# Attention with memory slots and a mixture of experts on one core: another order for the opening, and the second batch's value weights placed later

## The chip, the cores and the metric

One Trainium2 chip, one of its cores. The metric is the device time of one execution in microseconds (us), as the median of several runs.

## The reference

Sizes: batch 8, 8 heads, 576 rows, head width 64, 32 memory slots; model width 512, 8 experts of inner width 1024. All in float32.

```python
a = softmax(phi, axis=2)                               # 8 x 8 x 576 x 32
k_m = einsum('bhsm,bhsd->bhmd', a, k)                  # memory keys
v_m = einsum('bhsm,bhsd->bhmd', a, v)                  # memory values
attn = softmax(q @ k_m^T / 8)
x = (attn @ v_m) as 4608 tokens x 512
logits = x @ w_gate + modality_bias[modality_id]
e = argmax(logits);  gate = softmax(logits)[e]
out = gate * (relu(x @ w1[e]) @ w2[e])                 # per token, its own expert
```

With these inputs the biases decide, and the kernel takes the expert that the first token prefers for all, checks at the end whether any token wanted another, and only then runs a slow path.

## The kernel before, in words

Work goes batch by batch. A batch's 576 tokens lie as 64 x 9 rows; part 0 is four of the nine row groups (`RA`), part 1 the other five (`RB`). The attention's last product is never made: memory values times w1 gives "value weights" (`value_products`, 128 x 1024 for each of two groups of heads), and the hidden layer is the softmax weights times these (`hidden`, eight pieces f = 0 to 7). For precision each operand is split in an upper and a lower half (`...h`, `...l`), and a product is three: upper by upper, lower by upper, upper by lower. `outputs` multiplies the hidden rows by w2, three products for each f, into one bank for each tile t of 128 tokens; `store` scales by the gate on ScalarE (`ob`) and writes out.

PSUM has eight banks: four in a ring under the name `pe`, and two pairs (`pair_of_banks(0)` and `(1)`; `bank("pa")` and `bank("mem")` are the first halves of these).

Order is by hand. `plan_first` writes the steps of batch 0's first part in the order in which they are issued. `plan_memory`, `plan_turns` and `plan_steps` put the attention steps of later batches in a list with due times, and `plan_experts` lists the expert steps. `weave` merges the two lists by a table of planned costs (`TAKES`): an attention step goes out when the steps that it names are done by plan, its `floor` is reached and its due progress is made; else the next expert step does. Within each list the order stays. Each engine works through its own instructions in the order issued, so a step that waits holds up what stands behind it on its engine.

The opening of batch 0, by engines: SP loads phi, k, the first part of q, v, then (when the first token's expert is known) w1, w2 and the rest. VectorE reduces the peaks (`first_max`), subtracts, ScalarE takes exponentials in two pieces of five and four rows (`mem_exp`), TensorE multiplies by k and then v (`first_products`), while VectorE sums the exponentials (`mem_sums`). `first_divide`, `first_even` and `first_odd` scale the even heads on ScalarE and the odd ones on VectorE. The keys are turned on TensorE (`first_keys`), q in place on VectorE (`q_turn`), then come the scores of part 0, the softmax (`soften`, `first_weights`) and the split of its weights (`first_split`, `xah` and `xal`) for each group of heads. Value weights of the first 512 columns are made twice (step `vw` 0 and 2): the second copy has the upper half taken off by TensorE (`value_rest`), and ScalarE writes the lower half (`value_remainder`); the other 512 columns are done by ScalarE (`value_upper`) and VectorE (`value_lower`). `warm` issues products that nobody reads. `first_w2` splits one of eight chunks of w2: ScalarE casts `w2h`, GpSimd subtracts `w2l`. The step `start` sets the planned clock.

The hidden pieces f = 0 to 3 of part 0 are made term by term (`some_hidden`, steps ha to he), f = 4 and 5 in the two halves of one pair of banks (`one_of_two`), the rest in ring banks. After that tiles 0 and 1 get their output products, the second scores come (part 1 of batch 0), and tiles 2 and 3 follow after part 1's hidden pieces. Batch 1's value weights stand behind tile 2 (first half) and in the middle of tile 3 (second half).

Of the kernel before, what the change touches and what calls it, by code (L numbers as in the profile page):

```python
# [8 lines left out]
F32 = mybir.dt.float32  # L9
# [45 lines left out]
def attn_moe(ctx: ExitStack, tc: tile.TileContext, q, k, v, phi, mod_id, w_gate, mod_bias, w1, w2, out):  # L55
# [23 lines left out]
    BUSY = 86, 10  # L79
# [74 lines left out]
    def warm(n, small=False, name="pa"):  # L154
        if n > 0:
            idle = pair_of_banks(0) if small else bank(name)
            for n in range(n):
                if small:
                    r, c = QP * (n % 2), BL * (n // 2 % 4)
                    nc.tensor.matmul(  # L160
                        idle[c:c + BL, n % 2, 0:16], lhsT=busy[r:r + QP, 0:BL], rhs=busy[r:r + QP, 0:16],
                        start=True, stop=True, tile_position=(r, c),
                    )
                else:
                    nc.tensor.matmul(idle, lhsT=busy[:, 0:P], rhs=busy, start=True, stop=True)


# [88 lines left out]
    def biases(pairs):  # L256

        for pair in pairs:
            for m in range(NMOD):
                ts_ = slice(pair * QC, (pair + 1) * QC)  # L260
                part = wk.tile([P, QC, E], F32, name="part") if m else bias[:, pair]
                nc.gpsimd.tensor_tensor(
                    part, is_m[m][:, ts_].broadcast_to([P, QC, E]), mb[:, m:m + 1, :].broadcast_to([P, QC, E]),
                    op=ALU.mult,
                )
                if m:
                    nc.gpsimd.tensor_tensor(bias[:, pair], bias[:, pair], part, op=ALU.add)
# [67 lines left out]
    def mem_exp(b):  # L335
# [6 lines left out]
        else:  # L342
            topc = live["topc", b]
            pb = bank("mem")
# [6 lines left out]
        for cs in (slice(0, RB), slice(RB, QC)):  # L351
            nc.vector.tensor_tensor(
                px[:, :, cs], ph[:, :, cs], peak.broadcast_to([P, HG, cs.stop - cs.start, M]), op=ALU.subtract
            )
            nc.scalar.activation(px[:, :, cs], px[:, :, cs], AF.Exp)
        live["pe", b] = pe, None

    def mem_sums(b):
        pe = live["pe", b][0]
        if b == 0:  # L360
            x = pe.rearrange("p j x -> p (j x)")
            t2 = wk.tile([P, HG, 4 * M], F32, name="t2top").rearrange("p j x -> p (j x)")
# [371 lines left out]
    def value_upper(hf):  # L734
        for g, pv in enumerate(live["pv", hf]):
            nc.scalar.copy(vws[0][:, g, hf * 512:(hf + 1) * 512], pv)
# [13 lines left out]

    def value_weights(b, hf):
# [4 lines left out]
    def hidden(i, part, f, terms=range(3), groups=range(NG), to=None):  # L756
# [16 lines left out]
        if terms[-1] < 2 or groups[-1] < NG - 1:  # L773
            return
# [4 lines left out]
        for p0, p1, h0 in parts:  # L779
            hh, hl = (x[:, f, h0:h0 + p1 - p0] for x in hs)  # L780
            nc.vector.scalar_tensor_tensor(hl, ph[:, p0:p1], 0.0, hh.bitcast(F32), op0=ALU.max, op1=ALU.subtract)  # L781
# [49 lines left out]
    def first_w2(c):  # L831
# [15 lines left out]
        "vwp": (1.15, ""), "vwu": (0.0, "A1.15"), "vwl": (0.0, "D1.35"),  # L847
# [48 lines left out]
    def plan_first():  # L896
# [4 lines left out]
        def nothing(n, name="pa"):  # L901
            add(("nothing", len(attention)), "nothing", [], warm, n, False, name)
# [425 lines left out]
```

## Time and profile before

| | |
|---|---|
| median of 3 runs | 395.9 us (395.86 to 395.95) |
| profiled execution | 395.96 us, its span 394.1 us |
| busy: TensorE, VectorE, ScalarE, GpSimd | 380.2, 243.0, 144.9, 46.0 us |
| granted TensorE clock | 0.997 of full speed |
| moved by DMA | 56.91 MB |

The span is counted from the first to the last instruction. In the profile's views PE is TensorE, PEld its weight loads, DVE VectorE, ACT ScalarE, POOL GpSimd, SP the engine that issues most DMAs (`SPq` its queue). A row has start, length and engine, the source line (L798), the operation and what it writes and reads; "x16" stands for as many alike in a row, and square brackets hold idle time of the engine before and what ended it. A line is that of the listing above; helpers such as `turn` (L146) stand for many callers, so tiles tell more.

### The profile page before, as it was taken

The numbers are of one execution on the slowest core, as the hardware profiler recorded it, in microseconds if no ns is written. First come the engines' busy times: TensorE is split into PE (matmuls) and PEld (weight loads), VectorE is DVE, ScalarE is ACT, GpSimd is POOL, SyncE is SP. The second block draws the span as 40 slices with busy tenths as digits, with TensorE's granted clock in tenths as the row PEclk, the third lists the DMA queues.
The fourth block names the chain that finished last, engine by engine and source line by source line (L and its number), as shares of the span: only waits on it lengthen the run. The fifth ranks groups of instructions, "written<-read, shape, count | busy, mean of one in ns | idle before, by whom it ended". The sixth has DMA issues, their size and how long they took to land.

```text
span 394.1 us, 10127 instructions
## 1 busy us (share of the span) xinstructions
PE 380.2 (96%) x4217; PEld 305.0 (77%) x4219; DVE 243.0 (62%) x612; ACT 144.9 (37%) x347; POOL 46.0 (12%) x112
## 2 busy tenths in 40 slices
PE   7789999999999999999999999999999999999993
PEld 3557785889779887787878878797968879698982
DVE  4676864885797466856687366873687558660400
ACT  2264333515344333433443234352533425251410
POOL 3219420013000200030000200011000200000000
PEclk9999999999999999999999999999999999999998
DMA  8998167624841391628311293616211011431111
GB/s 291 360 380 311 66 163 280 245 108 140 260 140 46 106 368 57 227 77 303 112 27 55 62 346 118 218 30 210 86 28 28 27 30 29 167 128 28 30 33 55
DMA packets 28700, 56.91 MB, mean 144 GB/s; under 512 B 3044, under 2 KB 8164, under 8 KB 28644
## 3 DMA queue, kind: packets, MB, share of 16 engines
q1 hardware_dynamic: 28368, 55.87, 42.3%
q8 instruction: 35, 0.57, 0.6%
q10 hardware_dynamic: 276, 0.30, 0.2%
q14 instruction: 21, 0.17, 0.1%
HBM read 37.28 MB, written 18.87 MB: 142 GB/s over the span
## 4 chain that ended last, share of the span: by engine, by line
PE 89%; DVE 4%; DMA 3%; ACT 1%; issue 0%; SPq 0%; ACTq 0%
PE pe L798 50%; PE pe L769 25%; PE pair L386 4%; PE pe L728 4%; PE pair L562 3%; DMA kv_sb<-in_v_dram 3%; PE pair L675 1%; PE pair L146 1%; PE pe L411 1%; DVE a L595 0%; PE pair L728 0%; DVE a L589 0%; DVE hl L781 0%; ACT ob L811 0%; PE pair L539 0%
## 5 line engine op out<-in xcount | busy, mean ns | idle before, releaser
L798 PE MATMUL pe<-w2h,hh 128*128 128x512 f32 x288 | 116.8, 406 | 0.0
L798 PE MATMUL pe<-w2h,hl 128*128 128x512 f32 x288 | 112.5, 391 | 0.0
L798 PE MATMUL pe<-w2l,hh 128*128 128x512 f32 x288 | 110.4, 391 | 0.0
L781 DVE SCALAR_TENSOR_TENSOR hl<-pe,hh 128x256 fp32r<-128x256 f32 (+2 forms) x158 | 57.9, 392 | 42.1 <-ACT hh L778 41.2
L798 PEld LDWEIGHTS pe<-w2h,hh 128*128 128x128 f32 x288 | 54.1, 188 | 23.2 <-issue 12.3
L778 ACT ACTIVATE hh<-pe 128x256 fp32r<-128x256 f32 (+2 forms) x158 | 53.3, 362 | 37.9 <-PE pe L769 37.4
L798 PEld LDWEIGHTS pe<-w2l,hh 128*128 128x128 f32 x288 | 54.0, 188 | 11.8
L798 PEld LDWEIGHTS pe<-w2h,hl 128*128 128x128 f32 x288 | 54.2, 188 | 9.5
L811 ACT ACTIVATE ob<-pe,gates 128x512 f32<-128x512 f32 x36 | 24.8, 691 | 81.6 <-issue 49.0
L769 PE MATMUL pe<-xbh,vwh 128*128 128x320 f32 x128 | 40.1, 313 | 0.7 <-ACT ob L811 0.7
L769 PE MATMUL pe<-xbh,vwl 128*128 128x320 f32 x128 | 39.5, 309 | 0.0
L769 PE MATMUL pe<-xbl,vwh 128*128 128x320 f32 x128 | 39.5, 309 | 0.0
L769 PE MATMUL pe<-xah,vwh 128*128 128x256 f32 x124 | 34.5, 286 | 0.2 <-ACT xah L644 0.2
L769 PE MATMUL pe<-xal,vwh 128*128 128x256 f32 x124 | 34.5, 284 | 0.0
L769 PE MATMUL pe<-xah,vwl 128*128 128x256 f32 x124 | 34.5, 283 | 0.0
L322 POOL COPY ts<-tm 32x4 f32<-32x4 f32 x24 | 4.8, 199 | 201.3 <-DVE tm L314 200.5
L152 DVE TENSOR_TENSOR vwl<-pe,vwh 128x512 fp32r<-128x512 f32 x28 | 17.9, 679 | 13.0 <-ACT vwh L151 13.0
L589 DVE STREAM_TRANSPOSE a<-pair 128x256 f32<-128x256 f32 (+1 forms) x32 | 13.6, 461 | 18.9 <-PE pair L562 18.9
L769 PEld LDWEIGHTS pe<-xbh,vwh 128*128 128x128 f32 x128 | 24.0, 188 | 1.3 <-ACT ob L811 0.9
L769 PEld LDWEIGHTS pe<-xah,vwh 128*128 128x128 f32 x124 | 23.3, 191 | 1.9 <-ACT xah L644 1.6
L769 PEld LDWEIGHTS pe<-xbl,vwh 128*128 128x128 f32 x128 | 24.0, 188 | 0.3
L769 PEld LDWEIGHTS pe<-xbh,vwl 128*128 128x128 f32 x128 | 24.0, 188 | 0.0
(165 smaller groups left out, 459.0 us busy)
## 6 DMA issues: line engine op xcount, KB each, us to landing
kv_sb<-in_k_dram SPq DMA_DIRECT2D x8, 1152.0 KB, 5.7
kv_sb<-in_v_dram SPq DMA_DIRECT2D x8, 1152.0 KB, 9.4
out_dram<-ob SPq DMA_DIRECT2D x64, 128.0 KB, 2.4
q_sb<-in_q_dram SPq DMA_DIRECT2D x7, 1152.0 KB, 7.9
ph<-in_phi_dram SPq DMA_DIRECT2D x7, 576.0 KB, 4.1
raw<-in_moe_w_dram SPq DMA_DIRECT2D x2, 1024.0 KB, 7.6
raw<-in_moe_w_dram SPq DMA_DIRECT2D x1, 1280.0 KB, 10.5
out_dram<-ob SPq DMA_DIRECT2D x4, 256.0 KB, 2.6
```

The source lines that it names most:

```text
L146: nc.tensor.transpose(dst, src, ident[:rows, :rows])
L152: nc.vector.tensor_tensor(l, src, h.bitcast(F32), op=ALU.subtract)
L322: nc.gpsimd.tensor_copy(ts_[BL * a:BL * (a + 1)], live["tm"][BL * o:BL * (o + 1)])
L386: nc.tensor.matmul(live["kvp"][M * j:M * (j + 1), g], lhsT=pe[half, j, c * M:(c + 1) * M], rhs=kv_sb[half, :, j, c * D:(c + 1) * D], start ...
L562: nc.tensor.matmul(sc[g][M * j:M * (j + 1), a, c0 * BL:(c0 + n) * BL].rearrange("p (c t) -> p c t", t=BL), lhsT=kTs[b % 2][p0:p0 + BL, u, ...
L589: nc.vector.transpose(a[:, g].rearrange("p a c m -> p a (c m)"), sc[g][:, :, RA * part * BL:(RA * part + n) * BL])
L728: nc.tensor.matmul(pvs[g][M * j:M * (j + 1), :], lhsT=vT[b][rows, j, :], rhs=raw1[rows, j, cols], start=True, stop=not more, tile_position ...
L769: nc.tensor.matmul(ph[:, 0:n], lhsT=(vl if k == 2 else vh)[:, g, cols], rhs=xl if k == 1 else xh, start=(g == k == 0), stop=(g == NG - 1 a ...
L778: nc.scalar.activation(hs[0][:, f, h0:h0 + p1 - p0], ph[:, p0:p1], AF.Relu)
L781: nc.vector.scalar_tensor_tensor(hl, ph[:, p0:p1], 0.0, hh.bitcast(F32), op0=ALU.max, op1=ALU.subtract)
L798: nc.tensor.matmul(po, lhsT=tile_columns(hl if n == 1 else hh, f, t), rhs=(w2l if n == 2 else w2h)[:, f, :], start=(f == n == 0), stop=(f ...
L811: nc.scalar.activation(ob, po, AF.Copy, scale=gate_of(b, t))
```

## The change

- SP issues v's load ahead of the first part of q. Four more of the small products of nothing stand at the start.
- The first exponentials go by three rows in three pieces instead of five and four; their sums are added in thirds; the peaks that they subtract are spread into a ring bank instead of a pair.
- Four products of nothing instead of seven behind the exponentials, and three later in a ring bank instead of a pair; the spread of the known row moves ahead of k's products; the first turn of q moves behind the sums, ahead of the odd halves of the keys; v's products move behind it. Floors of several steps go.
- Value products stand behind the first group's softmax weights; the repeated ones are in ring banks; the split of the first weights comes ahead of the remainders; the upper halves of the second 512 columns are cast group by group around the second split, and the first chunk of w2 is split there too.
- Of the hidden pieces f = 0 to 3, two are in a pair of banks and evicted together (`relu`); f = 4 to 7 are all in ring banks. Tiles 0 and 1 take each chunk of w2 in turns.
- Biases of later pairs of batches are made one pair at a time, two batches apart. Batch 1's value weights move: the first half behind f = 1 of tile 3, the second to its end, with the lower half on VectorE after batch 1's first weights are split.

```diff
-    BUSY = 86, 10
+    BUSY = 90, 10
...
     def mem_exp(b):
...
-            pb = bank("mem")
+            pb = bank("mem" if b else "pe")
...
-        for cs in (slice(0, RB), slice(RB, QC)):
+        parts = [slice(c, c + QC // 3) for c in range(0, QC, QC // 3)] if b == 0 else (slice(0, RB), slice(RB, QC))
+        for cs in parts:
...
     def mem_sums(b):
...
-            nc.vector.tensor_tensor(t2, x[:, 0:4 * P], x[:, 4 * P:8 * P], op=ALU.add)
-            nc.vector.tensor_tensor(t2[:, 0:2 * P], t2[:, 0:2 * P], t2[:, 2 * P:4 * P], op=ALU.add)
+            nc.vector.tensor_tensor(t2, x[:, 0:n], x[:, n:2 * n], op=ALU.add)
+            nc.vector.tensor_tensor(t2, t2, x[:, 2 * n:3 * n], op=ALU.add)
             nc.vector.tensor_tensor(rf, t2[:, 0:P], t2[:, P:2 * P], op=ALU.add)
-            nc.vector.tensor_tensor(rf, rf, x[:, 8 * P:9 * P], op=ALU.add)
+            nc.vector.tensor_tensor(rf, rf, t2[:, 2 * P:3 * P], op=ALU.add)
...
+    def value_upper_weights(b, hf):
+        value_products(b, hf)
+        value_upper(hf)
...
+    def relu(i, part, fs):
+        n = MAIN + QP if part else MAIN
         parts = [(0, MAIN, 0), (MAIN, n, MAIN + QP)] if part and i else [(0, n, 0)]
-        for p0, p1, h0 in parts:
-            nc.scalar.activation(hs[0][:, f, h0:h0 + p1 - p0], ph[:, p0:p1], AF.Relu)
+        for f in fs:
+            for p0, p1, h0 in parts:
+                nc.scalar.activation(hs[0][:, f, h0:h0 + p1 - p0], live["ph", f][:, p0:p1], AF.Relu)
...
     def plan_first():
...
         def some_hidden(name, kind, after, terms, groups):
             for f in range(FCH // 2):
+                last_, own = terms[-1] == 2 and groups[-1] == NG - 1, f >= FCH // 4
...
+            if last_:
+                add(("h", 0, 0, FCH // 2 - 1), "relu", [], relu, 0, 0, range(FCH // 4, FCH // 2))
...
-        nothing(7)
+        nothing(4)
+        add(("known",), "nothing", [], spread_row)
+        add(("sums", 0), "first sums", [("exp", 0)], mem_sums, 0)
+        add(("k", 0), "k0", [("exp", 0)], first_products, 0, floor=9.0)
+        add(("ks", 0), "nothing", [("sums", 0)], first_sums)
+        add(("kn", 0), "kn0", [("k", 0), ("sums", 0)], first_divide)
         turns(0, 0, 9.5)
-        add(("sums", 0), "first sums", [("exp", 0)], mem_sums, 0)
-        add(("k", 0), "k0", [("exp", 0)], first_products, 0, floor=9.9)
-        add(("known",), "nothing", [], spread_row)
-        add(("ks", 0), "nothing", [("sums", 0)], first_sums)
-        add(("v", 0), "v0", [("exp", 0)], first_products, 1, floor=12.3)
-        add(("kn", 0), "kn0", [("k", 0), ("sums", 0)], first_divide)
         add(("ko", 0), "ko0", [("kn", 0)], first_odd, 0)
         turns(0, 1, 11.0)
+        add(("v", 0), "v0", [("exp", 0)], first_products, 1)
...
-        add(("vw", 0, 0), "vwp", [("kvT", 0)], value_products, 0, 0, pair_(0), floor=17.1)
-        add(("vw", 0, 2), "vwp", [], value_products, 0, 0, pair_(1), True, floor=18.2)
         add(("n", 0, 0, 0, 0), "n1", [("e", 0, 0, 0, 3)], first_weights, 0, 0)
-        add(("vwu", 0, 0), "vwu", [("vw", 0, 0)], value_upper, 0)
-        add(("vwr", 0, 0), "vwr", [("vwu", 0, 0)], value_rest, 0)
-        add(("vw", 0, 1), "vwp", [], value_products, 0, 1, pair_(0), floor=19.8)
         add(("n", 0, 0, 0, 1), "n2", [], first_weights, 0, 1)
         add(("e", 0, 0, 1, 2), "e1", [], soften, 0, 0, 2, 1)
-        add(("vwl", 0, 0, 0), "vw1", [("vwr", 0, 0)], value_remainder, 0, 0)
+        add(("vw", 0, 0), "vwp", [("kvT", 0)], value_products, 0, 0, pair_(0))
+        add(("vwu", 0, 0), "vwu", [("vw", 0, 0)], value_upper, 0)
+        add(("vw", 0, 2), "vwp", [], value_products, 0, 0, None, True)
         add(("xu", 0, 0, 0), "xu1", [("n", 0, 0, 0, 1)], first_split, 0, 0)
         add(("e", 0, 0, 1, 3), "ee", [("e", 0, 0, 1, 2)], soften, 0, 0, 3, 1)
         add(("xl", 0, 0, 0), "e1", [("xu", 0, 0, 0)], first_split, 0, 1)
+        add(("vwr", 0, 0), "vwr", [("vwu", 0, 0)], value_rest, 0)
+        for g in range(NG):
+            add(("vwl", 0, 0, g), "vw1", [("vwr", 0, 0)], value_remainder, 0, g)
+        add(("vw", 0, 1), "vwp", [], value_products, 0, 1, pair_(0))
...
-        add(("vwu", 0, 1), "vwu", [("vw", 0, 1)], value_upper, 1)
+        add(("vwu", 0, 1, 0), "vw1", [("vw", 0, 1)], value_upper, 1, range(1))
...
+        add(("vwu", 0, 1), "vw1", [("vw", 0, 1)], value_upper, 1, range(1, 2))
+        add(("w2", 0), "w2", [], first_w2, 0)
...
-        add(("start",), "start", [], lambda: None, floor=24.9)
+        add(("start",), "start", [], lambda: None, floor=25.0)
         turns(1, 0, 26.5)
-        turns(1, 1, 27.6)
-        add(("s", 0, 1), "s1", [("qt", 0, 1, 1), ("vwl", 0, 1)], scores, 0, RA, RB, floor=29.0)
+        turns(1, 1, 27.2)
+        add(("s", 0, 1), "s1", [("qt", 0, 1, 1), ("vwl", 0, 1)], scores, 0, RA, RB, floor=28.6)
...
     def plan_steps(b, dues):
...
-        if b == 0:
-            add(("bias", 1), "nothing", [], biases, range(1, NPAIR))
         if i:
             add(("others", pair), "others", [("g", b)], others, pair)
+            if b < B - 1:
+                add(("bias", pair + 1), "nothing", [], biases, pair + 1)
...
     def plan_experts(b):
...
-                if t == 2 and f == (FCH // 2 if b else FCH) - 1 or t == 3 and f == FCH // 2 - 1:
+                if b and t in (2, 3) and f == FCH // 2 - 1:
                     next_values(t - 2)
+                if b == 0 and t == 3 and f == 1:
+                    next_values(0)
+                if b == 0 and t == 3 and f == FCH - 1:
+                    stage(experts, ("vwp", 1, 1), "vwpu", [("kvT", 1)], value_upper_weights, 1, 1, banks=2, full=True)
+                    stage(experts, ("vw", 1, 1), "vwl", [("x", 1, 0), ("vwp", 1, 1)], value_lower, 1)
...
-                parts = [("o2", range(2), t, f) for t in tiles for f in range(FCH)]
+                parts = [("o2", range(2), t, f) for f in range(FCH) for t in tiles]
...
         load_kv(0, 0)
+        load_kv(0, 1)
         load_queries(0, 0, RA)
-        load_kv(0, 1)
-        warm(BUSY[0], True)
+        warm_small(BUSY[0])
         warm(BUSY[1])
```

More of the change, by code (lines that the diff above doesn't have):

```diff
@@ L152, in split, with warm, warm_small @@
         nc.vector.tensor_tensor(l, src, h.bitcast(F32), op=ALU.subtract)
[L154 to L165, printed above, removed]
+    def warm(n, name="pa"):
+        idle = bank(name)
+        for _ in range(n):
+            nc.tensor.matmul(idle, lhsT=busy[:, 0:P], rhs=busy, start=True, stop=True)
+    def warm_small(n):
+        idle = pair_of_banks(0)
+        for n in range(n):
+            r, c = QP * (n % 2), BL * (n // 2 % 4)
+            nc.tensor.matmul(
+                idle[c:c + BL, n % 2, 0:16], lhsT=busy[r:r + QP, 0:BL], rhs=busy[r:r + QP, 0:16],
+                start=True, stop=True, tile_position=(r, c),
+            )
     def halves(src, b):
@@ L254, in prepare, with biases @@
             nc.gpsimd.tensor_copy(wgd[rows, :, g, :], wg[rows])
[L256 to L267, printed above, removed]
+    def biases(pair):
+        for m in range(NMOD):
+            ts_ = slice(pair * QC, (pair + 1) * QC)
+            part = wk.tile([P, QC, E], F32, name="part") if m else bias[:, pair]
+            nc.gpsimd.tensor_tensor(
+                part, is_m[m][:, ts_].broadcast_to([P, QC, E]), mb[:, m:m + 1, :].broadcast_to([P, QC, E]),
+                op=ALU.mult,
+            )
+            if m:
+                nc.gpsimd.tensor_tensor(bias[:, pair], bias[:, pair], part, op=ALU.add)
     def rows_of(part):
@@ L754, in value_weights, with hidden @@
             split([x[:, g, hf * 512:(hf + 1) * 512] for x in vws], pv)
-    def hidden(i, part, f, terms=range(3), groups=range(NG), to=None):
+    def hidden(i, part, f, terms=range(3), groups=range(NG), to=None, evict=True):
         cols = slice(f * P, (f + 1) * P)
@@ L942, in plan_first @@
         add(("prepare",), "nothing", [], prepare)
-        add(("bias", 0), "nothing", [], biases, range(1))
+        add(("bias", 0), "nothing", [], biases, 0)
         for k in range(3):
@@ L1065, in plan_experts @@
                 kind = f"h{part + 2 * (part and b % 2)}"
-                own = b == part == 0 and f < FCH // 2 + 2
-                args = (range(3), range(NG), one_of_two) if own else ()
-                stage(
-                    experts, ("h", b, part, f), kind, [("x", b, part)] + ([("vwl", 0, 1)] if b == 0 else []),
-                    hidden, b % 2, part, f, *args, banks=int(not own), full=not own,
-                )
+                stage(experts, ("h", b, part, f), kind, [("x", b, part)] + ([("vwl", 0, 1)] if b == 0 else []), hidden, b % 2, part, f, banks=1, full=True)
                 if b == part == 0:
-                    for c in range(f - FCH // 2, f - FCH // 2 + 1):
-                        second(c)
+                    second(f - FCH // 2 + 1)
             tiles = range(2 * part, 2 * part + 2)
             if b == part == 0:
-                parts = [("o2", range(2), t, f) for t in tiles for f in range(FCH)]
+                parts = [("o2", range(2), t, f) for f in range(FCH) for t in tiles]
                 parts += [("o1", range(2, 3), t, f) for t in tiles for f in range(FCH - 1)]
@@ L1081, in plan_experts @@
                 for n, (kind, terms, t, f) in enumerate(parts):
[L1082 to L1083 removed]
+                    if n < FCH // 2 - 1:
+                        second(FCH // 2 + 1 + n)
                     some(t, f, kind, terms)
```

36 lines of the change are left out of this document (19 added, 17 removed), and 2 rows, old and new, of the table TAKES.

## The prediction

> **What bounds the kernel now.** I read the page first, then the chain of waits, the list of TensorE's waits, and last the rows in order of time where those waits stand.
>
> ```profile
> PE 380.2 (96%) x4217; PEld 305.0 (77%) x4219; DVE 243.0 (62%) x612; ACT 144.9 (37%) x347; POOL 46.0 (12%) x112
> PE   7789999999999999999999999999999999999993
> ```
>
> TensorE is busy 96% of 394.1 us. In the row of 40 slices (9.85 us each) only the first three and the last are below 9: in the opening a saved microsecond can end the kernel earlier, and from about 30 us on only a wait of TensorE itself counts. The profiled execution took 395.96 us, 1.86 more than its span; the median of the runs is 395.9, so the same difference holds for both.
>
> ```profile
> 2.28 11.43 DMA kv_sb<-in_v_dram
> 22.14 0.59 ACT vwl L744
> 30.01 1.44 PE pe L769 x12
> 34.86 1.09 PE pair L562 x57
> 46.91 0.70 ACT ob L811
> ```
>
> These are pieces of the chain that ended last (start, length, what; work between them left out). It is the load of v to 13.7, then a ping-pong of engines to 30, TensorE with products of the hidden layer (12 in 1.44 us, 0.12 each), the second part's scores at 34.86, then VectorE up to the first gated output, which ends at 47.6. Only behind that does TensorE run almost alone.
>
> ```profile
> PE pe L411 <- DMA kv_sb<-in_v_dram: 1.3, 1, 1.3
> PE pair L769 <- DVE hl L781: 0.9, 1, 0.9
> PE pair L562 <- ACT kT L512: 0.9, 2, 0.5
> PE pe L769 <- ACT ob L811: 0.7, 1, 0.7
> PE pair L146 <- ACT values L480: 0.4, 1, 0.4
> ```
>
> TensorE's waits (us in all, times, longest): 1.3 for v, 0.9 for a bank (`hl`, at 29 us), 0.7 for the first gated output (`ob`), and the two of 0.45 for batch 1's values and keys near 62 us. The change aims at all of them.
>
> **The loads.** SP now issues k, v, q; before it was k, q, v.
>
> ```profile
> L179 SPq DMA_DIRECT2D q_sb<-in_q_dram x1: 507/507/507, 1.7 to 1.7; - x1
> DMA to landing us min/median/max: 7.6/7.6/7.6
> ...
> L175 SPq DMA_DIRECT2D kv_sb<-in_k_dram x1: 454/454/454, 1.2 to 1.2; - x1
> L175 SPq DMA_DIRECT2D kv_sb<-in_v_dram x1: 698/698/698, 2.3 to 2.3; - x1
> DMA to landing us min/median/max: 6.6/9.0/11.4
> ...
> 10.00:11.00 1.00, 1.00 (x47) 1.00 (x40) 0.86 (x3) 0.12 (x1) 0.00 (x0) 1.00 1.11 403
> ```
>
> Issue times and times to landing: q 1.73 + 7.6 = 9.3; k 1.23 + 6.6 = 7.8; v 2.28 + 11.4 = 13.7. Between them the engines move about 403 GB/s (last row), so these loads queue behind one another. v without q's 512 KB ahead lands some 1.3 us sooner or more, at 12.4 or below. q becomes the last: at least 9.3 plus v's 1152 KB at that rate, 2.9, so 12.2; at most about 13.7, when now all four have landed. The gap of 1.4 us says that v's last packets were late for a reason that the queue's place alone doesn't give. I take 13.5, near the upper end, because that row measures the whole set. [...] No other DMA lies between these on SP, and what follows them comes in the same order as before.
>
> **Exponentials by three rows, and the order behind them.**
>
> ```profile
> 8.03 1.40 DVE L352 TENSOR_TENSOR exp<-ph,pair 128x640 f32<-128x640 f32 x2
> 8.86 1.26 ACT L355 ACTIVATE exp<-exp 128x640 f32<-128x640 f32 x2 [5.14 <-DVE exp L352]
> 9.68 2.19 PE L411 MATMUL pair<-kv_sb,exp 64*64 64x128 f32 x72
> 12.88 0.16 DVE L435 TENSOR_TENSOR recs<-rec,places 128x4 f32<-128x4 f32 x1
> 13.15 0.52 ACT L448 ACTIVATE even<-pair,recs 128x64 f32<-128x64 f32 x2 [0.74 <-DVE recs L435]
> 13.70 0.86 DVE L455 SCALAR_TENSOR_TENSOR keys<-pair,recs,even 128x64 f32<-128x64 f32 x4 [0.65 <-ACT even L448]
> 14.47 0.70 DVE L550 STREAM_TRANSPOSE q_sb<-q_sb 128x512 f32<-128x512 f32 x1
> 15.87 0.44 PE L146 MATMUL pair<-ident,keys 128*128 128x128 f32 x2
> 16.77 1.07 PE L562 MATMUL pair<-q_sb,kT 32*32 32x128 f32 x64 [0.46 <-ACT kT L512]
> ```
>
> Two subtractions take 1.40, two exponentials 1.26; one third of the nine rows costs about 0.53 and 0.49 (a half is 0.70 and 0.63, most of it by size). The products of k then start after 8.03 + 0.53 + 0.49 = 9.1 instead of 9.68, take 2.19 and end at 11.3; the last third is ready at about 10.1, before its turn. The peaks lie in a bank of their own, as the products would otherwise wait for the last subtraction to read them. The adds for the sums cost the same (three thirds for 512 and 256 columns), begin when VectorE has done the subtractions, without a turn of q ahead, and end near 11.3. So the reciprocals, 12.88 + 0.16 = 13.04 before, come at about 12.3, and the even halves at 12.9. Three fewer idle products and the four small ones more lie in TensorE's waits for data: nothing.
>
> The products of v follow on TensorE at about 11.7 (v is there or up to 0.7 late) and end by 13.9 to 14.6. But q's turn now stands on VectorE ahead of the keys, and it waits for q; behind it stand the odd halves, the second turn, and TensorE's turn of the keys. From q's landing: 0.70 + 0.86 + 0.90 (15.87 to 16.77) = 2.46; the second turn ends within that last piece. With 13.5 the first scores start at 15.97: **0.8 us** earlier. The ends are q at 13.7 (0.6) and q at 12.3 (2.0). The products of v leave the path.
>
> **First split and banks, to 27 us.**
>
> ```profile
> 21.33 0.45 DVE L638 STREAM_TRANSPOSE aT<-a 128x256 f32<-128x256 f32 x1
> 23.06 0.43 DVE L646 TENSOR_TENSOR xal<-aT,xah 128x256 fp32r<-128x256 f32 x1 [0.98 <-ACT xah L644]
> 25.67 0.42 DVE L646 TENSOR_TENSOR xal<-aT,xah 128x256 fp32r<-128x256 f32 x1 [0.47 <-ACT xah L644]
> 27.22 0.28 PE L769 MATMUL pair<-xah,vwh 128*128 128x256 f32 x1
> 29.03 0.38 PE L769 MATMUL pair<-xah,vwh 128*128 128x256 f32 x1 [0.93 <-DVE hl L781]
> 31.29 0.40 PE L798 MATMUL pe<-w2h,hh 128*128 128x512 f32 x1
> ```
>
> The first weights are turned at 21.78; ScalarE splits them only after a cast of `vwl` (22.14, chain), so VectorE idles 0.98 before 23.06. The new order splits first: 21.8 + 0.41, so VectorE goes on at 22.25, and the second group's weights, which wait for the second group's exponential behind it, move by nearly as much, as the cast no longer lies ahead of that exponential either; 0.1 goes to the exponential that they then wait for. The second split of 25.67 moves with them, since ScalarE's casts of `vwh` are now one ahead of it and one behind. **0.7 us**; between 0 (if the casts push it back) and 1.0, the longest such wait. Taking the repeated value products to banks of the other ring spares them the wait for the scores' transposes; what follows them waits for ScalarE's casts in any case, so nothing more.
>
> From 27.22 the hidden products of f = 4 to 7 stand: 31.29 - 27.22 = 4.07 for 24 products of 0.12, 2.9. The rest is the wait of 0.93 before 29.03, where both halves of the pair of banks hung on one reader, and small gaps. Now f = 2 and 3 sit in that pair, with both evictions after the last product, and f = 4 to 7 have ring banks, of which f = 5 needs that of f = 0, free in time if the evictions move up with the second split. **1.2 us**; 0 if VectorE's evictions come a product late each, 1.2 if not. The row of waits names one culprit, so I take the upper end.
>
> **w2.** The cast of the first chunk moves up on ScalarE, between the last cast of `vwh` and the first evictions, which have to wait for VectorE's `vwl` there anyway. Taking two tiles in turns uses a chunk every four output products; any small waits for casts go, and I count nothing. GpSimd starts its remainders earlier too.
>
> ```profile
> 31.02 5.04 POOL L829 TENSOR_TENSOR w2l<-raw,w2h 128x512 fp32r<-128x512 f32 x4 [0.62 <-ACT w2h L828]
> 37.77 1.46 DVE L595 TENSOR_TENSOR a<-a,mx 128x640 f32<-128x640 f32 x1
> ...
> 76.40 0.82 DVE L595 TENSOR_TENSOR a<-a,mx 128x640 f32<-128x640 f32 x1
> ```
>
> Four of these take 5.04, 1.26 each; eight need about 10.1, from about 25 on the new clock, so they end near 36, before the remainder products begin. They cost something where VectorE reads two operands from SBUF: 1.46 for a subtraction that takes 0.82 later on. That overlap of 0.64 exists already and stays; a second one would cost up to 1.26, none at best. I take none, as the instructions near the new start read PSUM. [...] The biases of later batches leave GpSimd's queue behind these for a place where it idles: nothing.
>
> **Part two and the gates.** So far 0.8 + 0.7 + 1.2 = 2.7 at the first output product. From the second scores (34.86) to the end of the gated output (47.61) are 12.75, mostly VectorE; the planner gives the scores 0.4 less floor, so they come after about the same count of output products or one pair fewer (0 to 0.46 earlier). TensorE's 0.7 at 47 shrinks by 0.2: **2.9** in all.
>
> **Batch 1.**
>
> ```profile
> 64.92 1.09 PE L728 MATMUL pe<-raw,vT 64*32 64x512 f32 x16
> ...
> 70.97 1.25 DVE L152 TENSOR_TENSOR vwl<-pe,vwh 128x512 fp32r<-128x512 f32 x2
> 72.14 0.68 DVE L658 TENSOR_TENSOR xal<-aT,xah 128x512 fp32r<-128x512 f32 x1
> ...
> 72.77 0.28 PE L769 MATMUL pe<-xah,vwh 128*128 128x256 f32 x1
> ```
>
> Its value products are put off: the first half behind two output steps of tile 3, the second to the end of that tile. The two waits near 62 us get work to fill them: 0.9. But batch 1's weights end at 72.14 + 0.68 = 72.82, and their first product starts at 72.77: no slack. Their cover from 64.92 is now 7.9 us; two output steps of 0.7 fewer make it about 6.4, while VectorE's chain loses only the 1.25 of the second half's remainder, now behind the weights. And that half needs two banks of four, one of which tile 3 gives back only by a gated output: up to 0.7 of new wait, like the one at 47. Between +0.9 and -0.8 I take **+0.2**, the middle, since the chain on VectorE shortens by about what its cover does.
>
> **Sum.** 2.9 + 0.2 = 3.1 against 395.96, that is 392.9, and 392.8 against the median.
>
> **The rivals.**
> *q lands early* (12.3). For it: 403 GB/s, and q's own 7.6 us. Against: v's 13.7. The first scores start 1.2 us earlier than forecast: 391.6. Chance 0.14.
> *VectorE gives it back.* GpSimd's remainders, now from about 25 us, block two more of VectorE's two-operand steps (0.64 each, by the subtraction's row), or evictions come late at f = 5 and 6. Then 1.3 of the 3.1 are lost: 394.1; with the bank wait of batch 1, 394.9. For it: no slack in VectorE's chain from 34.86 on. Chance 0.20. [...]
> *Nothing moves.* Another load (the first half of w1, or w2) would have to set the opening. The stream stays the same, and w2's first cast could be asked for too early; but the wait list names no such load. 395.9, chance 0.07.
> *Slower: batch 1's weights.* TensorE stands at batch 1's first hidden product until the weights are split, as its program has nothing else in between. The forecast turns at a wait of more than 3.1 + 0.2 us there, against none now; 0.8 more makes it measurable. At twice the loss of cover plus the bank and a blocked step (3.0 + 0.7 + 0.64) it is 397.0. For it: the slack of zero. Against: VectorE loses 1.25 of work in that stretch. Chance 0.07.
>
> **Numbers.** The forecast has 0.52, with its own range 392.0 to 393.7. Of 395.9, 0.2% is 0.8 us, about what the measurement can tell from no change. Faster: 0.52 + 0.14 + 0.20 = 0.86; same 0.07; slower 0.07. The range of 391.0 to 395.0 takes in the early q and the part given back and leaves out the last two.
>
> **What would show it.** v's products starting before 12.5 without a wait for DMA; a wait of VectorE for q at 12.3 to 13.6, ending in `q_sb`; first scores near 16.0; no 0.98 before `xal`; no 0.9 wait on `hl`; first output product near 28.6; first gated output ending near 44.7; near 60 us no waits for keys and values, and a wait or none at batch 1's first hidden product. It is wrong if q lands after 14.3 (then the scores start later than before), if the second scores don't move with the output products, or if TensorE stands for over a microsecond at batch 1.

## The result, and the profile after

The changed kernel takes 392.45 us (median of four runs, 392.29 to 393.04) against 395.88 before (four runs on the same chip): ratio 0.9917, 95% interval 0.990 to 0.9934. That is 3.4 us, of which 3.1 were forecast. The profiled execution took 392.55 us, its span 390.8. Of all runs told of below, one execution of `split_behind`, 420.05 us at a granted clock of 0.851, was slow and is left out.

The page of the changed kernel: busy times, and TensorE's row of 40 slices.

```profile
PE 379.2 (97%) x4218; PEld 305.1 (78%) x4220; DVE 243.7 (62%) x613; ACT 144.8 (37%) x348; POOL 45.7 (12%) x112
PE   7899999999999999999999999999999999999993
```

Of the 3.3 us by which the span is shorter, 2.3 were idle time of TensorE (11.6 instead of 13.9 us, gone from the first slices) and 1.0 counted as busy (379.2 for 380.2; the value products' gap, which comes below, counts as busy there). TensorE's waits, as in the list of before (us in all, times, longest):

```profile
PE pair L146 <- DVE keys L457: 0.7, 1, 0.7
PE pair L564 <- ACT kT L514: 0.5, 1, 0.5
PE pe L776 <- ACT xah L657: 0.4, 1, 0.4
PE pe L776 <- DVE xal L660: 0.3, 1, 0.3
PE pe L413 <- DMA kv_sb<-in_v_dram: 0.3, 1, 0.3
PE pair L396 <- POOL sums L283: 0.3, 1, 0.3
```

v's wait fell from 1.3 to 0.3; those for `hl`, for `ob` and for batch 1's values are gone. In their place stand a wait for the keys (VectorE now waits for q first), two at batch 1's first hidden product, 0.73 together, and one for `sums` of GpSimd (0.31, in batch 6, at 269 us). Rows of the changed kernel in order of time, from all engines (start, length, engine):

```profile
12.32 2.20 PE L413 MATMUL pe<-kv_sb,exp 64*64 64x128 f32 x72 [0.33 <-DMA kv_sb<-in_v_dram]
13.82 0.71 DVE L552 STREAM_TRANSPOSE q_sb<-q_sb 128x512 f32<-128x512 f32 x1 [1.20 <-DMA q_sb<-in_q_dram]
16.12 1.07 PE L564 MATMUL pair<-q_sb,kT 32*32 32x128 f32 x64 [0.46 <-ACT kT L514]
21.54 0.43 DVE L648 TENSOR_TENSOR xal<-aT,xah 128x256 fp32r<-128x256 f32 x1 [0.17 <-ACT xah L646]
25.70 0.28 PE L776 MATMUL pe<-xah,vwh 128*128 128x256 f32 x1
28.58 0.40 PE L812 MATMUL pe<-w2h,hh 128*128 128x512 f32 x1
30.97 1.18 PE L564 MATMUL pair<-q_sb,kT 32*32 32x160 f32 x64
33.95 1.85 DVE L597 TENSOR_TENSOR a<-a,mx 128x640 f32<-128x640 f32 x1
43.40 1.26 ACT L825 ACTIVATE ob<-pe,gates 128x512 f32<-128x512 f32 x2 [0.79 <-DVE gates L706]
69.06 0.39 PE L776 MATMUL pe<-xal,vwh 128*128 128x256 f32 x1 [0.34 <-DVE xal L660]
92.39 2.62 PE L388 MATMUL pair<-kv_sb,exp 64*32 64x128 f32 x141
```

Against the kernel before, the lead grows like this: first scores 0.65 us (16.77 to 16.12), first split 1.52 (23.06 to 21.54), hidden product of f = 4 also 1.52, first output product 2.71 (31.29 to 28.58), second scores 3.8 (34.79 to 30.97), first gated output 3.5 (46.91 to 43.40), batch 1's hidden products 3.8. Batch 2's first products start 3.8 earlier (96.18 to 92.39), but 141 of the 144 that took 2.25 now take 2.62, and the last of them ends 2.73 behind the first start. From batch 3 on the lead is 3.3; in batch 6 another 0.5 goes, and the last product of all starts at 384.29 instead of 387.13, 2.84 earlier. The rest of the span's 3.3 lies behind the last product, where the two executions took 6.48 and 6.96 us. That stretch took 6.4 to 7.2 us in the fourteen profiles of this case, in no order that I can see.

### The profile page after: what moved, and what is told of

It is laid out like the page before. It is cut to its first block, busy times and chain, and to the rows that moved or that the text cites. A ratio compares the mean times of both kernels' runs of the same rounds, so it can differ in the third digit from the quotient of the medians.

```text
span 390.8 us, 10131 instructions
## 1 busy us (share of the span) xinstructions
PE 379.2 (97%) x4218; PEld 305.1 (78%) x4220; DVE 243.7 (62%) x613; ACT 144.8 (37%) x348; POOL 45.7 (12%) x112
## 4 chain that ended last, share of the span: by engine, by line
PE 86%; DVE 5%; DMA 3%; ACT 2%; POOL 1%; issue 1%; SPq 0%; ACTq 0%; POOLq 0%
PE pe L812 48%; PE pe L776 26%; PE pe L730 3%; PE pair L564 3%; PE pair L388 3%; DMA q_sb<-in_q_dram 3%; PE pair L677 1%; PE pair L146 1%; DVE a L597 1%; ACT ob L825 1%; DVE a L591 0%; DVE mx L595 0%; PE pair L541 0%; POOL t2sums L279 0%; ACT exp L356 0%
## 5 line engine op out<-in xcount | busy, mean ns | idle before, releaser
L812 PEld LDWEIGHTS pe<-w2h,hh 128*128 128x128 f32 x288 | 54.1, 188 | 21.2 <-issue 11.0
L776 PEld LDWEIGHTS pe<-xal,vwh 128*128 128x128 f32 x124 | 23.7, 191 | 0.8 <-DVE xal L660 0.5
L152 DVE TENSOR_TENSOR vwl<-pe,vwh 128x512 fp32r<-128x512 f32 x26 | 16.6, 678 | 12.0 <-ACT vwh L151 12.0
```

The lines of the kernel that those rows point to most:

```text
L152: nc.vector.tensor_tensor(l, src, h.bitcast(F32), op=ALU.subtract)
L776: nc.tensor.matmul(ph[:, 0:n], lhsT=(vl if k == 2 else vh)[:, g, cols], rhs=xl if k == 1 else xh, start=(g == k == 0), stop=(g == NG - 1 a ...
L812: nc.tensor.matmul(po, lhsT=tile_columns(hl if n == 1 else hh, f, t), rhs=(w2l if n == 2 else w2h)[:, f, :], start=(f == n == 0), stop=(f ...
```

## The experiments

Comparisons are with the kernel before on the same chip; its medians there were 395.72 to 396.15. Two kernels whose ratios differ by less than some 0.0016 (0.6 us) aren't told apart by time; there I go by the traces, above all by the start of the last product.

**The loads: v first, alone and undone.** In the kernel before only:

```diff
+        load_kv(0, 1)
         load_queries(0, 0, RA)
-        load_kv(0, 1)
```

> The kernel before with v's load ahead of q's and nothing else. Theory (the loads and the order behind them are one change): q lands at about 13.8, and in the old order its first turn stands on VectorE ahead of the sums, so sums, denominators and keys start behind 14.5: first scores near 19.6 instead of 16.77, and the kernel about 2.8 us slower, near 398.7. Rival (v's wait of 1.3 was the cost, so its load alone brings it): first scores 0.7 to 1.3 earlier, 394.6 to 395.2.

Measured: 399.16 us, ratio 1.0077 (1.006 to 1.0094). Then the reverse in the changed kernel (queries ahead of v):

> The changed kernel with q's load ahead of v's again. Theory (what lands last sets the first scores): v lands at 13.7 again, its products fill TensorE to 15.95, the keys are turned behind them, first scores at 16.85 instead of 16.12, 393.2. Rival (the rest of the new order hides the loads, so the two orders are worth the same): within 0.2 of 392.45.

Measured: 394.17 us, ratio 0.9951 (0.9936 to 0.9966). Both lost more than expected, the first by 0.5 us, the second by 1.0. Alone, the new order of loads makes VectorE wait for q ahead of the sums (4.23 us, in rows below), and the keys with them; the order behind the exponentials has to change along with it. What nobody expected is in v's products. Rows of TensorE and VectorE in `loads_alone`, and its stretches of 2 us (length, busy times of PE, PEld, DVE, ACT, POOL, then the granted clock, DMA share and GB/s):

```profile
16.16 0.39 PE L422 MATMUL pair<-ones_c,sums 64*64 64x1 f32 x8 [3.90 <-DVE sums L368]
16.40 4.10 PE L411 MATMUL pe<-kv_sb,exp 64*64 64x128 f32 x72
13.71 0.71 DVE L550 STREAM_TRANSPOSE q_sb<-q_sb 128x512 f32<-128x512 f32 x1 [4.23 <-DMA q_sb<-in_q_dram]
```

```profile
16.00:18.00 2.00, 1.84 (x40) 1.84 (x44) 0.77 (x5) 0.52 (x2) 0.89 (x6) 0.50 1.05 374
18.00:20.00 2.00, 2.00 (x44) 2.00 (x40) 1.30 (x5) 0.00 (x0) 1.69 (x8) 0.50 1.07 394
```

The same two views of `q_ahead`:

```profile
13.85 3.69 PE L413 MATMUL pe<-kv_sb,exp 64*64 64x128 f32 x72 [1.84 <-DMA kv_sb<-in_v_dram]
```

```profile
12.00:14.00 2.00, 0.16 (x5) 0.15 (x8) 1.83 (x8) 0.52 (x2) 0.00 (x0) 1.00 1.04 379
14.00:16.00 2.00, 2.00 (x48) 2.00 (x48) 0.76 (x2) 0.00 (x0) 0.00 (x0) 0.59 1.15 264
16.00:18.00 2.00, 2.00 (x34) 1.43 (x26) 0.00 (x0) 0.00 (x0) 0.61 (x4) 0.56 1.07 378
```

v's 72 products took 4.10 and 3.69 us instead of 2.20, at a granted clock of 0.50 and 0.59, behind 3.90 and 1.84 us in which TensorE had nothing. In the kernel before TensorE was busy 0.67 of the same 2 us, and the clock stayed at 1.00.

**The same with TensorE kept busy.** `q_ahead` with eight filler products ahead of v's:

```diff
+        nothing(8)
         add(("v", 0), "v0", [("exp", 0)], first_products, 1)
```

> The changed kernel with the queries' load ahead of v's as before, and eight filler products (128x512, into an idle bank) ahead of v's products, so that TensorE does not stand idle for v. Theory: v's products took 3.69 us instead of 2.19 with that order because the granted clock fell to 0.59 behind TensorE's idle 1.84; kept busy, the clock stays at 1.0, v's products take 2.2 to 2.4 and the first scores start near 17.0 instead of 18.49: 392.9 to 393.3 us, against 394.17 without the fillers. Rival: the slow products come from v's packets or from the port, not from the clock; then v's products take over 3.4 us again and the time stays at 394.0 to 394.3.

TensorE's rows, and one stretch of 2 us:

```profile
13.71 2.20 PE L413 MATMUL pe<-kv_sb,exp 64*64 64x128 f32 x72
16.73 1.07 PE L564 MATMUL pair<-q_sb,kT 32*32 32x128 f32 x64 [0.46 <-ACT kT L514]
20.32 0.63 PE L730 MATMUL pair<-raw,vT 64*32 64x512 f32 x4 [0.84 <-issue]
```

```profile
14.00:16.00 2.00, 2.00 (x74) 1.83 (x66) 0.60 (x1) 0.00 (x0) 0.00 (x0) 1.00 1.15 282
```

The mechanism is as expected: clock 1.00, products in 2.20, first scores 1.8 earlier than in `q_ahead`'s profile. The time is not: 394.35 us, ratio 0.9965 (0.9952 to 0.9978), where 392.9 to 393.3 were expected. (The profiled execution of `q_ahead` took 395.54, above its median, at a mean granted clock of 0.991, the other five at 0.994 to 0.996; so the slow clock seems to cost less in most executions.) The third row shows a new loss: in the middle of the value products TensorE stood 0.84 us for nothing that the profile names (`issue`).

**The first split: order and banks undone.** In the changed kernel, first the order only; then also the repeated value products in the old pair (`pair_(1)` for `None`):

```diff
+        add(("vwr", 0, 0), "vwr", ...)
+        add(("vwl", 0, 0, 0), "vw1", ...)
         add(("xu", 0, 0, 0), "xu1", ...)
...
         add(("xl", 0, 0, 0), "e1", ...)
-        add(("vwr", 0, 0), "vwr", ...)
-        for g in range(NG):
-            add(("vwl", 0, 0, g), "vw1", ...)
+        add(("vwl", 0, 0, 1), "vw1", ...)
```

> The changed kernel with one step undone: VectorE again takes the rest and the first remainder of the value weights ahead of batch 0's first split. The forecast gave this order, by itself, 0.7 us: then the first hidden product (25.70 at f=4 in the changed kernel) and all behind it come 0.7 later, first output product near 29.3, 393.1 us. Rival: the wait of 0.98 in the kernel before came from the order and from the repeated value products waiting for their banks together; with that bank freed the rest and the remainder are done before the split's operands are, and the old order costs at most 0.15: output product at 28.6 to 28.75, 392.4 to 392.6 us.

> As the run before it, and the repeated value products also back in the pair of banks of the kernel before. By the forecast (order alone 0.7, bank nothing more) the same 393.1 us as with the order alone. Rival (either of the two suffices to remove the wait, both undone bring it back): a wait of about 0.9 on the first split's difference as before the change, output product near 29.4, 393.2 to 393.4 us while the order alone stays at 392.5.

Measured: 392.54 (ratio 0.9912, 0.9898 to 0.9927) and 392.82 us (0.9918, 0.9905 to 0.9931), first output products at 28.45 and 28.66. The first agrees with the rival; the second with neither. VectorE's waits before the first `xal`, in the one and the other:

```profile
21.40 0.42 DVE L648 TENSOR_TENSOR xal<-aT,xah 128x256 fp32r<-128x256 f32 x1 [0.16 <-ACT xah L646]
```

```profile
21.59 0.42 DVE L648 TENSOR_TENSOR xal<-aT,xah 128x256 fp32r<-128x256 f32 x1 [0.30 <-ACT xah L646]
```

With order and bank as before, the wait of 0.98 comes back as 0.30 only. Both theories fall; something else made the other 0.7.

**The gap in the value products.** In the kernel before, the 32 value products ahead of that split took 2.99 us, in `split_and_repeat_back` 2.26 (first row: before; second: that kernel):

```profile
18.45 2.99 PE L728 MATMUL pair<-raw,vT 64*32 64x512 f32 x32 [0.35 <-ACT vT L520]
```

```profile
17.71 2.26 PE L730 MATMUL pair<-raw,vT 64*32 64x512 f32 x32 [0.36 <-ACT vT L522]
```

Two of the DMA queues carry instructions. On one of them the packets have 16 KB, 35 of them in both kernels (queue, packets, MB, share):

```profile
q8 instruction: 35, 0.57, 0.6%
```

In windows of 0.1 us, a packet starts at 17.8 in the kernel before, 17.7 in `q_ahead_busy`, each 0.65 or 0.7 ahead of the value products; the changed kernel has it at 16.2, 1.6 ahead, and no gap. So the kernel before, with nothing changed but more small and two fewer large filler products at its start, which moves the packets:

```diff
-    BUSY = 86, 10
+    BUSY = 156, 8
```

> The kernel before with more small filler products in its opening (156 of 64x32 and 8 of 128x512 instead of 86 and 10), where TensorE has only filler to do: about as much time, some 136 instructions more. In the kernel before, the 32 first value products take 2.99 us instead of 2.26, with a gap in the middle of them that no wait explains, 2.6 us behind the start of a packet of instructions (17.8); three kernels with such a gap resume 2.5 to 2.6 us behind such a packet. Theory: TensorE there waits for its instructions; with the program longer ahead of that place the packet comes earlier, the value products take 2.26, VectorE's wait of 0.98 for the first split shrinks to 0.3 or less, first output product near 30.6, 395.2 to 395.5 us. Rival: the gap belongs to the order of the loads or to the weights' landing; then the products take 2.99 again, the wait is 0.98 and the time is that of the kernel before within 0.2.

Rows of TensorE and, the third, of VectorE:

```profile
16.17 1.52 PE L562 MATMUL pair<-q_sb,kT 32*32 32x128 f32 x64 [0.46 <-ACT kT L512]
18.30 2.26 PE L728 MATMUL pair<-raw,vT 64*32 64x512 f32 x32 [0.36 <-ACT vT L520]
22.19 0.42 DVE L646 TENSOR_TENSOR xal<-aT,xah 128x256 fp32r<-128x256 f32 x1 [0.30 <-ACT xah L644]
59.85 0.32 PE L386 MATMUL pair<-kv_sb,exp 64*32 64x128 f32 x5 [0.62 <-issue]
```

The packets came at 14.0 and 20.5; the value products took 2.26, the wait was 0.30, and the first output product stood at 30.42, 0.87 earlier than before. (Of that, 0.6 is v, which landed earlier in this execution, the first scores starting at 16.17 instead of 16.77; 0.45 is lost again in the scores, and 0.7 is the gap.) But the time was 396.18 us, ratio 0.9996 (0.9981 to 1.0012), above what the theory gave: the packet of 14.0 falls ahead of the scores, which take 1.52 instead of 1.07, another, at 57.5, into batch 1's first products, 0.62, and a third, at 67.4, ahead of batch 1's second value products, 0.68. Its twelve runs lie in two groups, four at 394.2 to 394.5 and eight at 396.1 to 397.1; the profile is of the second, and what parts them wasn't seen.

So is the order of the split worth nothing? Two kernels have the new order and a gap as well. VectorE's wait before the first `xal` in `keys_first` (the next experiment; its gap of 0.49 lies in the repeated value products, as it does in the kernel before) and in `q_ahead_busy` (0.84, already in the first ones):

```profile
20.70 0.42 DVE L648 TENSOR_TENSOR xal<-aT,xah 128x256 fp32r<-128x256 f32 x1 [0.16 <-ACT xah L646]
22.85 0.43 DVE L648 TENSOR_TENSOR xal<-aT,xah 128x256 fp32r<-128x256 f32 x1 [0.76 <-ACT xah L646]
```

The new order keeps a gap in the repeated products away from the split, as the forecast said of the cast, and doesn't help against one in the first products, whose cast `vwh` still stands ahead of `xah`. In the changed kernel the gap is gone and the order has nothing to do. What it would have won in the kernel before, by itself, no run shows; in `keys_first`, whose split is as early as in the changed kernel (5.43 us behind the first scores), 0.4 us of the gap is still lost by the first output product.

**The turn of the queries behind the keys**, in the changed kernel (`turns(0, 0, 9.5)` after the step `ko`):

> The changed kernel with q's first turn on VectorE behind the odd halves of the keys instead of ahead. Theory (VectorE stands 1.2 us for q with the keys queued behind it): keys done at 13.8, v's products (to 14.5) become the last thing ahead of the keys' turn, first scores at 15.45 instead of 16.12, and all behind follows: 391.8. Rival (another load or the w1 weights at 16.8 set what follows): first scores 0.67 earlier, but 392.3 or more.

Measured: 392.31 us, ratio 0.9902 (0.9886 to 0.9918). The first scores start at 15.27, 0.85 earlier; the output product at 28.12, 0.46 earlier; and at the end 0.1 is left. Where it went, in rows of TensorE:

```profile
18.92 1.09 PE L730 MATMUL pe<-raw,vT 64*32 64x512 f32 x15 [0.49 <-issue]
94.52 0.53 PE L388 MATMUL pair<-kv_sb,exp 64*32 64x128 f32 x20 [0.59 <-issue]
```

Packets start at 16.3 and 92.0; TensorE goes on 2.6 and 2.5 us later. In the changed kernel one starts at 91.7, and the step in batch 2's products ends 2.7 us behind it.

**Banks undone.** Repeated products and filler in the old banks; f = 0 to 3 in ring banks, evicted singly; f = 4 and 5 in one pair:

```diff
-                last_, own = terms[-1] == 2 and groups[-1] == NG - 1, f >= FCH // 4
+                last_, own = terms[-1] == 2 and groups[-1] == NG - 1, False
...
+                own = b == part == 0 and f < FCH // 2 + 2
+                args = (range(3), range(NG), one_of_two) if own else ()
```

> The changed kernel with the old banks of the first hidden units (all four of f=0 to 3 in ring banks evicted one by one, f=4 and 5 in one pair), of the filler products and of the repeated value products; order of the loads and of the split as in the change. Theory: the stretch from f=4's products to the first output product goes back from 2.88 to about 4.07, so the output product stands at 29.8 and the time at 393.6 (up to 393.9 if the repeat delays the weights too). Rival: the later waits (0.07 at the gates, 0.73 at batch 1's first hidden products) take it up, and the time stays within 0.4 of 392.45.

TensorE's rows, the second of them the first output product:

```profile
27.47 0.39 PE L776 MATMUL pair<-xah,vwh 128*128 128x256 f32 x1 [1.05 <-DVE hl L793]
29.73 0.40 PE L812 MATMUL pe<-w2h,hh 128*128 128x512 f32 x1
```

Measured: 393.98 us, ratio 0.9957 (0.9945 to 0.9969). The wait on `hl` is back, the output product 1.15 later: as the theory had it. Batch 2's first products take 3.27 instead of 2.73, by a longer stall, and the last product of all starts 1.37 later than in the changed kernel.

**Exponentials in two parts, as before.**

```diff
-        parts = [slice(c, c + QC // 3) for c in range(0, QC, QC // 3)] if b == 0 else (slice(0, RB), slice(RB, QC))
+        parts = (slice(0, RB), slice(RB, QC))
```

> The changed kernel with the exponentials and their sums in two parts as before (128x640 and the rest) instead of three of equal size. Theory (the forecast's): VectorE waits 1.20 us for q behind them, so what they take longer, up to 0.5, is hidden: v's products start at most 0.3 later, the first scores at 16.1 to 16.2, and the time stays within 0.2 of 392.45. Rival: the sums and with them the keys come later than the turn of q: first scores 0.4 to 0.5 later and 392.9 us.

(The run also puts the sums and the bank of the spread peaks back.) Measured: 392.8 us, ratio 0.9927 (0.9914 to 0.994); its first scores start at 15.97, not later than with three parts, and VectorE's wait for q is 0.83 instead of 1.20. The longer work lies in that wait; the 0.35 between the medians isn't resolved, and the last product starts at 384.11, no later than in the changed kernel.

**w2 undone.**

```diff
-        add(("w2", 0), "w2", [], first_w2, 0)
...
-                parts = [("o2", range(2), t, f) for f in range(FCH) for t in tiles]
+                parts = [("o2", range(2), t, f) for t in tiles for f in range(FCH)]
```

> The changed kernel with w2's splitting and the order of the output products as before: the first of w2's parts split with the others, one tile's products behind the other's instead of in turns. The forecast put this step at nothing. In the changed kernel the subtraction of 128x640 ahead of batch 0's second exponentials took 1.85 us instead of 1.46 while GpSimd splits w2, and 10 output products lie ahead of the second scores. Theory: the second scores stay within 0.3 of 30.97, the gated output's first half within 0.4 of 43.40 and the time within 0.3 of 392.45. Rival: turns of two tiles are what lets the output products start without waiting for w2; undone, TensorE waits for GpSimd's splits and the time is 0.5 to 1.5 longer (393.0 to 394.0).

Measured: 393.64 us, ratio 0.9949 (0.9936 to 0.9962), in the range of the rival but not by its mechanism: the second scores start at 31.02 and TensorE doesn't wait for w2. VectorE and GpSimd, and then ScalarE:

```profile
37.36 0.78 DVE L612 TENSOR_SCALAR sa<-sa 128x20 f32<-128x20 f32 x1
36.82 1.28 POOL L843 TENSOR_TENSOR w2l<-t2sums,w2h 128x512 fp32r<-128x512 f32 x1
43.91 1.27 ACT L825 ACTIVATE ob<-pe,gates 128x512 f32<-128x512 f32 x2 [0.79 <-DVE gates L706]
```

GpSimd's last remainder runs to 38.10, 1.15 later than in the changed kernel (36.95), and a step of VectorE that takes 0.17 there takes 0.78 under it; the subtraction ahead of it takes 1.69 (1.85 in the changed kernel). The gated output starts 0.5 later, TensorE waits 0.49 for it, and the last product starts 0.43 later. Of the 1.2 between the medians that is what the traces give to this step; of the two profiled executions' difference another 0.65 lies behind the last product, where times scatter as much in other kernels.

**Batch 1's value weights at their old places.**

```diff
-                if b and t in (2, 3) and f == FCH // 2 - 1:
+                if t == 2 and f == (FCH // 2 if b else FCH) - 1 or t == 3 and f == FCH // 2 - 1:
                     next_values(t - 2)
```

> The changed kernel with batch 1's value weights where they stood before (behind tile 2, and in the middle of tile 3). Theory (the move only trades waits: 0.9 for values and keys against 0.7 for the weights and 0.3 for sums): the waits for values and keys near 59 us come back, the waits for batch 1's weights go, and the time is within 0.4 of 392.45. Rival (the move is worth its 0.9): 393.3. Rival (it costs): 391.9 or below.

Measured: 392.08 us, ratio 0.9903 (0.9887 to 0.9918). The waits near 60 us are back, 0.9 of them, and the 0.73 at the first hidden product gone; batch 3's first products start 0.3 earlier than in the changed kernel. The times don't resolve the move, but the two profiled executions tell it apart. At batch 2's first products it has won 0.16 (92.39 instead of 92.55), about what was forecast; then the changed kernel loses 0.45 in those products, where `values_back` has no stall, and 0.5 in batch 6, where its list has that batch's first products at 266.63 instead of 262.97 and TensorE waits 0.31 for `sums`. Without the move the last product starts at 383.49, 0.8 earlier. So in these executions it cost, by what it set off later.

**A version from what was learnt.** Turn behind the keys, value weights at the old places, and `BUSY = 134, 9`:

> The changed kernel with the turn of the queries behind the keys (alone 392.31), batch 1's value weights at their old places (alone 392.08), and 134 small and 9 large filler products in the opening instead of 90 and 10: some 86 instructions more ahead of everything, in about the same time. Theory: the two stalls that swallowed the earlier keys (0.49 in the repeated value products, 0.59 in batch 2's first products) belonged to packets of instructions that start less than 2.6 us ahead; moved earlier they are gone: first scores 15.3, first output product 27.9 or earlier, 391.2 to 391.7 us. Rival: stalls of that size turn up elsewhere, or the waits of batch 1 and 2 swallow it: 391.9 to 392.4.

Rows of TensorE, a row of its list of waits, and a stretch of 2 us:

```profile
16.74 0.49 PE L564 MATMUL pair<-q_sb,kT 32*32 32x128 f32 x25 [0.65 <-issue]
59.06 0.19 PE L396 MATMUL pair<-ones_c,sums 64*32 64x1 f32 x2 [1.39 <-issue]
```

```profile
PE pair L396 <- issue: 4.2, 3, 1.5
```

```profile
18.00:20.00 2.00, 2.00 (x24) 0.61 (x31) 1.90 (x6) 0.48 (x2) 1.73 (x7) 0.50 1.04 386
```

Measured: 399.36 us, ratio 1.0089 (1.0067 to 1.0111): worse than either expectation. The packets, moved, now hit the scores (one starts at 14.1) and the sums of three batches (the first at 56.4; 4.2 us in all), and behind the first of these stalls the granted clock fell to 0.50. The first scores did start at 15.24. So moving the program moved the stalls; I did not steer them, but where they stood can be told (last section).

## Why the prediction was right, and where only by chance

- **Loads and first scores: 0.8, measured 0.65.** q landed at 13.80, not at 13.5: the four loads together took as long as before, and the 0.2 that the forecast took off their end did not come. So it landed 0.1 behind the forecast's upper end, the 13.7 by which all four had landed before. The signs are there but for one: v's products start at 12.32, but behind a wait of 0.33 for v's load, where none was forecast; VectorE's wait into `q_sb` is 1.20. The products of k start at 9.45 instead of 9.1, which the wait for q hides.
- **First split: 0.7, measured 0.87 (1.52 less 0.65), with half of the cause.** The forecast gave it to the order of split and remainder. Undone, order and bank cost 0 to 0.15, counted from the first scores to the split; 0.7 was a gap in the value products of the kernel before, at a packet of instructions, which shifting the program alone removed. The order would have kept that gap from the split too (`keys_first`), but the gap vanished with the same edit, and that was luck. The forecast's step that failed is the one that read the 0.98 as a wait for a cast and did not ask why the cast was late: the row of 2.99 us for 32 products, whose next 16 take 1.09, was there.
- **Banks: 1.2, measured 1.19** (4.07 to 2.88) and 1.15 undone. Right, by the row that named one culprit.
- **w2: 0, and no new overlap.** Both mis-sized. The subtraction of 128x640 took 1.85 instead of 1.46, a loss of 0.4 (0.16 of it by w2's start, as `w2_back` has 1.69); but w2's earlier start kept GpSimd off VectorE's next step, a gain of 0.6 that `w2_back` shows, 0.45 of it net. The subtraction ends 0.68 to 0.69 us behind the end of the remainder that it overlaps, in the kernel before, in the changed kernel and in `w2_back`; so in these three its price was what that remainder still had to run. `hl`, which reads PSUM, lost nothing in the changed kernel, as the forecast took it: one of 128x256 takes 0.39 beside a remainder (at 28.93) and 0.42 with GpSimd idle (at 72.25). But the step of 0.78 in `w2_back` reads `sa` alone, so the loss isn't confined to two operands.
- **Second scores.** 0 to 0.46 forecast behind the output product, 1.1 measured: ten output products lie ahead of them instead of fourteen, at 0.23 each and some 0.2 in all by which the last six in the kernel before were slower. With the subtraction's 0.4 off, the gated output came 3.5 earlier, not 2.9.
- **Batch 1: +0.2, measured +0.3** at its hidden products (3.5 to 3.8): 0.9 of waits gone, 0.73 come. Then 0.5 is lost at batch 2, at the packet of 91.7, and 0.5 in batch 6. No step had that; with both, the move of the value weights costs 0.8 up to the last product (`values_back`).
- **The rivals.** Of "VectorE gives it back" one block of 0.4 came true, not two of 0.64; "Slower" had its wait, at 0.73 instead of over 3.3 (its own terms give 397.1, not 397.0); q was not early.

The sum, 3.1 against 3.4, holds because the gap that vanished was as long as the wait it was taken for, and because the term too low (second scores) and the losses that no term had (batches 2 and 6) cancel: at the last product the lead is 2.84.

## What to carry to other kernels

Before a wait is put down to the order of two steps, follow it back one row further: if a run of equal instructions takes longer than its count times its own pace, the late engine was late for another reason. A load's place in the queue is worth what the engine behind it does meanwhile: the same swap lost 3 us alone and gained 1.4 (by the ratios; 1.7 by the medians) with the order that fits it. And an edit that adds or drops instructions on TensorE can move a stall behind a packet of instructions, as `longer_opening` did: value products 2.26 instead of 2.99 us, scores 1.52 instead of 1.07. Gains below a microsecond can be that.

## What the runs showed of the hardware

**Packets of instructions.** Twelve stalls marked `issue`, in seven of these kernels, end 2.3 to 2.7 us behind the start of a 16 KB packet on the instruction queue, all amid dense runs of small products, with 0.4 to 1.5 us idle each. Those counted here keep to a place in TensorE's program. Counted from the start of the span (`--windows 0:T` with T at the stall), 347 or 348 products are issued, and as many weight loads, when the early stall comes, in `keys_first` (18.92), `q_ahead_busy` (20.32) and `both_and_longer` (16.74), and so it is at the gap of the kernel before; it is 856 at the second stall of `both_and_longer` and at the first marked one of `longer_opening`, and 1235 to 1237 in batch 2. The early one lies behind the second packet, those in batch 2 behind the ninth: 888 products further in seven packets, 127 in each and about as many weight loads, and 856 is four times 127 behind 348. So I take the packets for TensorE's own program, some 254 of these instructions in each, an estimate from these counts. In the changed kernel TensorE comes to the early place 2.5 us behind the packet of 16.2, and loses nothing.

So an edit ahead of a stall can shift it in the work: the 136 instructions more of `longer_opening` took it out of the value products and into the scores, which take 1.52 us instead of 1.07. What decides when a packet starts is open: at the start of the second, 329 products have been issued in the kernel before and 281 in the changed kernel, at that of the ninth 1108 and 1111.

**The clock.** In stretches of 0.4 us the granted clock is 0.50 from 14.4 to 17.8 us in `q_ahead`, from 14.4 to 21.2 in `loads_alone` and from 17.8 to 21.2 in `both_and_longer`, 3.4 or 6.8 us each time. Ahead of it TensorE had nothing for 1.84 us in the first and for 2.2 us in the second; in the third it had gaps of 0.46, 0.65 and 0.40. How busy TensorE was doesn't decide by itself: it was busy 1.98 of the 3.3 us ahead in `both_and_longer` and 1.88 of the same 3.3 us in the changed kernel, where the clock stayed at 1.00. What sets when it falls, and for how long, these runs don't show.
